# A transformer block on one core: attention's result turned by DMA in all sixteen tiles instead of six

## The chip, the core and the metric

The kernel runs on one core of a Trainium2 chip. The core has five engines that each work through their own queue in order: TensorE (PE; its weight loads are listed apart as PEld), VectorE (DVE), ScalarE (ACT), GpSimd (POOL) and SyncE (SP), which here does nothing but issue transfers. An engine whose next instruction waits does nothing else meanwhile. The metric is the time of one execution on the device in microseconds (us).

## The reference

The block has two parts, each with a residual: sliding-window attention (32 heads of 16 columns, each position looks at itself and at seven others two, four, ... fourteen positions back), then an MLP with a squared ReLU.

```python
S, D, H, Dh, W, dil, F = 2048, 512, 32, 16, 8, 2, 1792
q, k, v = heads_of(layernorm(x) @ wqkv)
logits = einsum("bhsd,bhswd->bhsw", q, k[window]) * Dh ** -0.5     # masked where pos < 0
o = einsum("bhsw,bhswd->bhsd", softmax(logits), v[window])
h = x + o.reshape(B, S, D) @ wo
r = relu(layernorm(h) @ w1 + b1)
out = h + (r * r) @ w2 + b2
```

All matrix products are made from values split into a high and a low part (a number = high + low): a product is the sum of high x high, low x high and high x low.

## The kernel before, in words

The 2048 positions are 16 tiles `t` of 128. Attention is made for pairs of tiles, `s = t // 2`. The MLP runs over groups of four tiles, `u = 0 ... 3`; `i = t % 4` is a tile's place in its group. While PE works on the QKV products of tiles 4 to 15 (`first_phase`) and then on the MLP of groups 0 to 2 (the loop over `u`), DVE and POOL make attention beside it; DVE multiplies and reduces (`dots`, `weigh`), and POOL sums the weighed values (`add_up`, L411).

Each tile goes this way: attention's result `o` (positions in partitions) is turned so that its columns lie in partitions, and split into `oh` and `ol`; the product with `wo` follows (`wo_product`, PE, into one of PSUM's banks); `h_add` (L639, DVE) adds the residual and starts the statistics of the second layernorm, either on DVE (`norm_stats`, L158 and L159) or, for the tiles in `AS`, on ACT (`act_stats`, L181 to L183); POOL finishes them with three small operations; ACT normalises (`h_norm`, L200, result `hn`); `hn` is turned and split into `hh` and `hl` for the MLP. `add_b2` (POOL) and `spill` (a DMA) put h aside until its group is finished.

There are two ways to turn a tile:

- on PE: `o_T` and `h_T` make four transposes into PSUM; ACT copies the high part from there (`hi_T`), DVE subtracts for the low part (`lo_T`, L150).
- by DMA, for the `o` of the tiles in `OV` and the `hn` of the tiles in `HV`: ACT sorts the halves of the 32-bit words into two planes (`turn_split`, L594, tile `pl`), SP issues a DMA transpose (`turn_dma`, L598), ACT puts the halves together again (`turn_join`, L603), and the split into high and low follows from there. `o_split` and `o_join` are these steps for `o`, `h_split`, `turn_join` and `h_parts` for `hn`.

The order of every engine's queue is written by a planner while the program is built. The program is a row of slots. In a slot first PE's work is written (the slot's body), then `end_slot` writes the tasks that are due in the slot (`at(delta, ...)`), then as many steps of attention as the planner thinks fit beside PE's work (`pump`), then the tasks that are to come behind them (`after(delta, ...)`):

```python
def end_slot(pe):
    now["pe"] += pe
    run(due)
    pump()
    run(late)
    now["slot"] += 1
```

`pump` goes on while DVE's planned time is less than PE's: `now["dve"] < now["pe"]`. Each step of attention is charged with its planned time times one of the factors in `SLOW` (first phase, u = 0, u = 1 and 2), the other work of DVE with `dve(...)`: 0.69 for a tile's `ol`, 0.7 for `h_add`, 0.93 for `norm_stats`, 1.0 for `HOLD`. PE is charged 0.44 for the transposes of a tile and 2.73 for a product. A weighed value's sum (`add_up`) is written only when the next step is drawn. `pump(until=s)` draws steps until attention of pair `s` is written in full.

In `first_phase` a slot is half a QKV product, and `k` counts the half-slots of its last two rounds from 0 (negative before). `OK`, `HK`, `OT`, `WO`, `HT` say at which `k` tile t's steps come. The x tiles 14 and 15 are normalised (ACT, `x_norm`) at k = 5 and 6 and transposed (PE, `x_T`) at k = 7 and 8. In this phase four PSUM banks take turns for the products.

In the loop over `u` a slot `p` holds one block `mlp1(u, f)` of the hidden layer (PE, tile `mm`, 12 matmuls), and from the fourth slot on `mlp2` (tile `acc`, 12 matmuls) of the block three slots earlier; p = 14 to 16 have `mlp2` alone. Two PSUM banks take turns for `mm`, `wo` and the transposes of this stage, so that a tile's bank is that of the one before the last. The relu that empties `mm` (`hidden`, L846, ACT) is due one slot later. `todo[p]` holds what a slot does for the next group's tiles: `OP`, `WP`, `HP` give the slots by `i`. Tiles with i = 0, 1 are split at p = 6, 7, joined two slots later, and multiplied with `wo` at p = 9, 10; tiles with i = 2, 3 are turned on PE at p = 12, 13 and multiplied at p = 13, 14 (for u = 2 one less).

Of the kernel before, what the change touches and what calls it, by code (L numbers as in the profile page):

```python
# [28 lines left out]
NEG = -4.0e9  # L29
ROWS = 15  # L30
LAG = 3
AS = (4, 5, 8, 9, 12, 13)
OV = (4, 5, 8, 9, 12, 13)
HV = (4, 5, 8, 9, 12, 13)
SLOW = 1.01, 1.10, 1.06
DELAY = 3
WJ = 2
XT = (9, 11), (7, 8)
OT = 4, 5, 10, 12
WO = 7, 9, 13, 15  # L40
HT = 20, 20, 21, 23
OK = (-6, -2, 4), (-5, -1, 5), (3, 6, 10), (4, 7, 12)
HK = (12, 15, 18), (14, 16, 19)
W2 = (18,)
LH = 3, 4, 10, 11
OP = 6, 7, 12, 13
# [12 lines left out]
def block_kernel(ctx, tc, x, wqkv, wo, w1, b1, w2, b2, out):  # L59
# [154 lines left out]
        for d, src in parts(tr, h_dst):  # L214
            hi(d, src)

    def lo_T(tr, h_dst, l_dst):
        for (d, src), h in zip(parts(tr, l_dst), h_dst):
            lo(nc.vector, d, src, h)
            dve(0.16 + 0.53 / len(h_dst))  # L220

    def mm3(ps, lh, ll, rh, rl, mid=None, at_=2 * KB, lows_last=False):

# [388 lines left out]
    def o_join(t):  # L612
        turn_join(("o", t))
        tr = planes.pop(("o", t))
        if t % R == RI:
            ohl = att.tile([P, 2, KB, P], F32R, name="ohl", tag="o", bufs=3)
            oT[t] = ohl[:, 0], ohl[:, 1]
        else:
            oT[t] = row("oh", (P, KB, P), F32R), row("ol", (P, KB, P), F32R)
        hi_T(tr, [oT[t][0]])  # L620
        after(0, lo_T, tr, [oT[t][0]], [oT[t][1]])

    def h_split(t):
        turn_split(("h", t), hn.pop(t))
# [33 lines left out]
    def wo_product(t, slots):  # L658
        ps = turn["mm"].tile("wo")
        oh, ol = oT.pop(t)  # L660
        mm3(ps, lambda k: oh[:, k, :], lambda k: ol[:, k, :],
            lambda k: wo_h[:, k, :], lambda k: wo_l[:, k, :], lows_last=t in OV)
        for n, (fn, a) in zip(slots, ((h_add, (t, ps)), (h_norm, (t,)), (add_b2, (t,)),
                                      (spill, (t,)))):
            (after if fn in (h_norm, spill) else at)(n + (fn is add_b2), fn, *a)

# [311 lines left out]
    def first_phase(t0):  # L980
        def chores(m):
            if t0 + 3 < 16:
                if m in (0, 2):
                    at(0, x_stats, t0 + 2 + m // 2)

                early = t0 == 12
                if m + early in (6, 7):
                    at(0, x_norm, t0 - 4 + m + early)
                if m in XT[early]:
                    x_T(t0 + 2 + XT[early].index(m))  # L990
            if t0 + 5 < 16 and m in (6, 9):
                at(0, load_x, t0 + 2 + m // 3)
            if jobs and m % 3 == 0:
                at(0, weight_job)
            k = t0 // 2 * 12 - 72 + m
            if k == 19:
                dve(HOLD)
            for t in range(R):
                if k == OT[t]:
                    at(0, load_h, t)  # L1000
                    if t not in OV:
                        o_T(t)
                if t in OV and k in OK[t]:
                    at(0, (o_split, lambda t: turn_dma(("o", t)), o_join)[OK[t].index(k)], t)
                if t in HV and k in HK[t]:
                    at(0, (h_split, lambda t: turn_dma(("h", t)),
                           lambda t: turn_join(("h", t)))[HK[t].index(k)], t)
                if k == WO[t]:
                    wo_product(t, (1, 3, 4, 6))
                    now["pe"] += 2.73  # L1010
                if k == HT[t]:
                    (at(0, h_parts, t) if t in HV else h_T(t))
            if k in W2:
                at(0, load_w2, W2.index(k))

        def half(m):
            end_slot(1.37)
            chores(m)

        for n in range(6):  # L1020
            chores(2 * n)
            qkv_of(t0 + n % 2, n // 2, lambda: half(2 * n + 1))
            end_slot(1.37)
# [41 lines left out]
    for u in range(R - 1):  # L1065
# [11 lines left out]
        for i in js:  # L1077
            t = R * (u + 1) + i
            if not end:
                a = i // 2 if u == 2 else 0  # L1080
                o0 = OP[i] - a
                if t in OV:
                    turned = [(o0, at, 0, o_split, t), (o0, after, 0, turn_dma, ("o", t)),
                              (o0 + 2, at, 0, o_join, t)]
# [26 lines left out]
        for p in range(FB + LAG):  # L1111
            more = 0.0
            if p == FB:
                run(due)
                dve(HOLD)
            if u < 2 and p == FB - 2:
                dve(HOLD)
            for fn, *a in sorted(todo.get(p, []), key=lambda x: x[0] is wo_product):
                fn(*a)
                more += 2.73 if fn is wo_product else 0.0  # L1120
            if p < FB:
                mlp1(u, fs[p])
                more += 2.73
                if first:
                    at(0, split_w2, p)
                    if p + 1 < FB:
                        load_w2(p + 1)
            q = p - LAG
            if q >= 0:
                f = fs[q]  # L1130
                mlp2(u, f, acc, js, q == 0, q == FB - 1,
                     (lambda: half(p)) if p in halves else None)
                more += 2.74
                if f < 12 and (need or first and p < FB - LAG):
                    free.append(place.pop(f))
                    if need:
                        at(1, fetch, need.pop(0))
            end_slot(more)
# [85 lines left out]
```

## Time and profile before

| | |
|---|---|
| median of 3 runs (lowest to highest) | 512.38 us (511.91 to 513.16) |
| profiled execution | 512.31 us, its span 510.5 us |
| PE busy | 501.9 us, 98% |
| DVE, POOL, ACT busy | 376.7, 351.2, 290.9 us |
| granted clock of PE, mean over the span | 0.999 |
| transposes of `o` on PE / by DMA | 40 in 10 tiles / 6 tiles |
| transposes of `hn` on PE / by DMA | 40 in 10 tiles / 6 tiles |

The span goes from the first to the last instruction. Busy times of different engines lie beside each other, and add up to more than the span. A row of a timeline or of the chain of waits begins with its start in us from the span's start and its length in us; a bracket at its end tells how long the engine was idle before it and whose work ended that. Rows of groups have the number of instructions, busy us and mean ns of one, and the idle time of the engine just before them.

### The profile page before, as it was taken

The page shows a single profiled execution, that of the slowest core. Times are in us where ns is not written, and L with a number is a line of the kernel's source. Part 1 is how long each engine was busy: PE and PEld are TensorE (multiplying, and loading weights), DVE is VectorE, ACT ScalarE, POOL GpSimd, SP SyncE. Part 2 cuts the span into 40 slices and gives each one's busy share as a digit, 9 for nine tenths or more (in the row PEclk, how much of TensorE's full clock was granted, in tenths as well). Part 3 has the DMA queues.
Part 4 walks back from the last instruction along what each step waited for, and adds up shares of the span by engine and source line. Part 5 has one row for each costly group of instructions (what it writes and reads, how often), then busy time and mean ns, then how long its engine had stood idle before and what let it go on. Part 6 is the DMA issues. An engine that isn't in the chain of part 4 may idle for free. (4 is left out here: it accounts for less than half of the span.)

```text
span 510.5 us, 7598 instructions
## 1 busy us (share of the span) xinstructions
PE 501.9 (98%) x2460; PEld 424.4 (83%) x2460; DVE 376.7 (74%) x512; ACT 290.9 (57%) x552; POOL 351.2 (69%) x430
## 2 busy tenths in 40 slices
PE   7999999999999999999999999999999999999997
PEld 6999788888888888888888878888888888998986
DVE  5479899988998899788879979899963046832233
ACT  4634686767434767485364557264564737666541
POOL 4714799895786798786778768776897364685610
PEclk9999999999999999999999999999999999999999
DMA  8678998989677889666587955767672172444112
GB/s 264 180 225 203 256 295 299 271 285 274 204 225 214 276 301 272 200 199 174 182 253 217 226 166 163 202 199 249 207 152 67 52 217 84 160 142 133 62 42 83
DMA packets 100912, 100.52 MB, mean 197 GB/s; under 512 B 21000, under 2 KB 69384, under 8 KB 100872
## 3 DMA queue, kind: packets, MB, share of 16 engines
q1 hardware_dynamic: 99928, 99.52, 65.4%
q10 hardware_dynamic: 944, 0.52, 0.3%
q8 instruction: 19, 0.31, 0.3%
q14 instruction: 21, 0.17, 0.1%
HBM read 72.65 MB, written 24.25 MB: 190 GB/s over the span
## 5 line engine op out<-in xcount | busy, mean ns | idle before, releaser
L411 POOL TENSOR_TENSOR pr<-pr 128x512 f32<-128x512 f32 (+1 forms) x128 | 132.5, 1035 | 45.7 <-DVE pr L354 40.3
L232 PE MATMUL mm<-big_l,w_h 128*128 128x512 f32 x336 | 88.7, 390 | 0.0
L354 DVE TENSOR_TENSOR pr<-ex,v 128x1024 f32<-128x1024 f32 x64 | 78.2, 1222 | 12.8 <-POOL o L411 6.5
L343 DVE TENSOR_TENSOR pr<-qp,k 128x1024 f32<-128x1024 f32 x64 | 76.9, 1202 | 5.6 <-ACT qp L272 5.5
L377 DVE TENSOR_REDUCE ex<-pr 128x64 f32<-128x1024 f32 x64 | 78.4, 1226 | 1.9
L232 PEld LDWEIGHTS mm<-big_l,w_h 128*128 128x128 f32 x336 | 62.8, 188 | 13.0
L150 POOL TENSOR_TENSOR rl<-r,rh 128x512 fp32r<-128x512 f32 x42 | 56.2, 1339 | 19.6 <-ACT rh L147 16.5
L232 PE MATMUL mm<-big_h,xl 128*128 128x512 f32 (+1 forms) x208 | 56.0, 379 | 0.2 <-DVE xl L150 0.2
L232 PE MATMUL mm<-big_h,xh 128*128 128x512 f32 (+1 forms) x208 | 53.5, 378 | 0.7 <-ACT xh L147 0.7
L232 PE MATMUL mm<-big_l,xh 128*128 128x512 f32 (+1 forms) x208 | 52.8, 375 | 0.0
L870 PE MATMUL acc<-big_l,rh 128*128 128x512 f32 x190 | 52.2, 390 | 0.0
L870 PE MATMUL acc<-big_h,rh 128*128 128x512 f32 x190 | 52.1, 391 | 0.0
L501 ACT COPY y<-mm 128x512 f32<-128x512 f32 (+1 forms) x52 | 28.6, 552 | 41.2 <-PE mm L232 33.0
L870 PE MATMUL acc<-big_h,rl 128*128 128x512 f32 x190 | 51.7, 389 | 0.0
L846 ACT ACTIVATE r<-mm,b_sb 128x512 f32<-128x512 f32 x42 | 28.8, 685 | 32.4 <-PE mm L232 32.3
L232 PE MATMUL mm<-big_l,w_l 128*128 128x512 f32 x168 | 45.0, 389 | 0.0
L232 PEld LDWEIGHTS mm<-big_h,xh 128*128 128x128 f32 x208 | 37.6, 188 | 7.0 <-ACT xh L147 1.5
L232 PEld LDWEIGHTS mm<-big_l,xh 128*128 128x128 f32 x208 | 38.2, 188 | 6.1 <-POOL big_l L150 0.2
L232 PEld LDWEIGHTS mm<-big_h,xl 128*128 128x128 f32 x208 | 37.2, 188 | 5.8 <-DVE xl L150 0.6
L870 PEld LDWEIGHTS acc<-big_h,rl 128*128 128x128 f32 x190 | 35.7, 188 | 7.5
L870 PEld LDWEIGHTS acc<-big_l,rh 128*128 128x128 f32 x190 | 35.5, 188 | 7.4
L870 PEld LDWEIGHTS acc<-big_h,rh 128*128 128x128 f32 x190 | 34.9, 188 | 6.7
(160 smaller groups left out, 904.1 us busy)
## 6 DMA issues: line engine op xcount, KB each, us to landing
k<-qkv_d SPq DMA_DIRECT2D x48, 288.0 KB, 2.8
v<-qkv_d SPq DMA_DIRECT2D x48, 288.0 KB, 3.2
qkv_d<-y SPq DMA_DIRECT2D x18, 512.0 KB, 4.2
big_l<-w2l_d SPq DMA_DIRECT2D x24, 256.0 KB, 3.0
xt<-in_A_x_dram SPq DMA_DIRECT2D x16, 256.0 KB, 4.6
q<-qkv_d SPq DMA_DIRECT2D x32, 128.0 KB, 4.7
h<-in_A_x_dram SPq DMA_DIRECT2D x16, 256.0 KB, 3.9
h_d<-h SPq DMA_DIRECT2D x16, 256.0 KB, 3.2
```

Of the source, the lines that this page charges most:

```text
L150: eng.tensor_tensor(out=dst, in0=src, in1=h, op=ALU.subtract)
L232: nc.tensor.matmul(ps, l(k), r(k), start=(n == 0), stop=(n == 3 * KB - 1))
L343: nc.vector.tensor_tensor(out=pr.rearrange("p i w h d -> p i w (h d)"), in0=qps["now"][:, j % 2].unsqueeze(2).to_broadcast([P, RI, W, GC]) ...
L354: nc.vector.tensor_tensor(out=p2, in1=vwin, op=ALU.mult, in0=e1[:, :, :, j * GH:(j + 1) * GH].unsqueeze(4).to_broadcast([P, RI, W, GH, DH]))
L377: nc.vector.tensor_reduce(out=lf[:, :, :, j * GH:(j + 1) * GH], in_=pr, axis=X, op=ALU.add)
L411: nc.gpsimd.tensor_tensor(out=dst, in0=p2[:, :, :w], in1=p2[:, :, w:2 * w], op=ALU.add)
L501: nc.scalar.copy(y[:, :, t % RI * GC:(t % RI + 1) * GC], ps[:, :j * GC].rearrange("p (j c) -> p j c", j=j))
L846: nc.scalar.activation(r, ps, AF.Relu, bias=b1_sb[:, f:f + 1])
L870: nc.tensor.matmul(acc[j], l[:, j * P:(j + 1) * P], w[f], start=(first and n < len(js)), stop=(last and n >= len(terms) - len(js)))
```

## The change

- `OV` holds all 16 tiles: the results of tiles 0 to 3, 6, 7, 10, 11, 14 and 15 are now turned by DMA too. `HV` has tiles 0 and 1 in addition. `AS` has tiles 0 to 3 in addition, so that their statistics are ACT's.
- `ol` of all tiles made by DMA is made by POOL (`lo_T` with `nc.gpsimd`), written behind the slot's attention steps.
- In `first_phase` the DMA follows the split in the same slot, behind the pump; `OK` and `HK` have two entries (split, join). Tiles 0 and 1 are split at k = -6, -5 and joined at 3, 4; tiles 2 and 3 are split at 3, 4 and joined at 10, 11.
- In the MLP loop tiles with i = 2, 3 are split two slots sooner than they were transposed (p = 10, 11) and joined where those transposes stood (p = 12, 13).
- The product with `wo` of these tiles comes behind `mlp1` of its slot and ahead of `mlp2`, instead of ahead of both. `h_add` of the tiles with i = 0, 1 comes behind the slot's attention steps; with i = 2, 3 it stays ahead of them. The order of a product's terms puts `ol` last for all tiles in `OV`.
- The factors in `SLOW` are 1.08 and 1.04 instead of 1.10 and 1.06 from u = 0 on.

```diff
@@ -29,18 +29,18 @@
 NEG = -4.0e9
 ROWS = 15
 LAG = 3
-AS = (4, 5, 8, 9, 12, 13)
-OV = (4, 5, 8, 9, 12, 13)
-HV = (4, 5, 8, 9, 12, 13)
-SLOW = 1.01, 1.10, 1.06
+AS = (0, 1, 2, 3, 4, 5, 8, 9, 12, 13)
+OV = tuple(range(16))
+HV = (0, 1, 4, 5, 8, 9, 12, 13)
+SLOW = 1.01, 1.08, 1.04
 DELAY = 3
 WJ = 2
 XT = (9, 11), (7, 8)
 OT = 4, 5, 10, 12
 WO = 7, 9, 13, 15
 HT = 20, 20, 21, 23
-OK = (-6, -2, 4), (-5, -1, 5), (3, 6, 10), (4, 7, 12)
-HK = (12, 15, 18), (14, 16, 19)
+OK = (-6, 3), (-5, 4), (3, 10), (4, 11)
+HK = (11, 18), (13, 19)
 W2 = (18,)
 LH = 3, 4, 10, 11
 OP = 6, 7, 12, 13
@@ -214,10 +214,11 @@
         for d, src in parts(tr, h_dst):
             hi(d, src)
 
-    def lo_T(tr, h_dst, l_dst):
+    def lo_T(tr, h_dst, l_dst, eng=nc.vector):
         for (d, src), h in zip(parts(tr, l_dst), h_dst):
-            lo(nc.vector, d, src, h)
-            dve(0.16 + 0.53 / len(h_dst))
+            lo(eng, d, src, h)
+            if eng is nc.vector:
+                dve(0.16 + 0.53 / len(h_dst))
 
     def mm3(ps, lh, ll, rh, rl, mid=None, at_=2 * KB, lows_last=False):
 
@@ -618,7 +619,7 @@
         else:
             oT[t] = row("oh", (P, KB, P), F32R), row("ol", (P, KB, P), F32R)
         hi_T(tr, [oT[t][0]])
-        after(0, lo_T, tr, [oT[t][0]], [oT[t][1]])
+        after(0, lo_T, tr, [oT[t][0]], [oT[t][1]], nc.gpsimd if t in tuple(range(16)) else nc.vector)
 
     def h_split(t):
         turn_split(("h", t), hn.pop(t))
@@ -662,7 +663,8 @@
             lambda k: wo_h[:, k, :], lambda k: wo_l[:, k, :], lows_last=t in OV)
         for n, (fn, a) in zip(slots, ((h_add, (t, ps)), (h_norm, (t,)), (add_b2, (t,)),
                                       (spill, (t,)))):
-            (after if fn in (h_norm, spill) else at)(n + (fn is add_b2), fn, *a)
+            late_ = fn in (h_norm, spill) or fn is h_add and t in OV and R <= t and t % R < RI
+            (after if late_ else at)(n + (fn is add_b2), fn, *a)
 
 
 
@@ -1001,10 +1003,17 @@
                     if t not in OV:
                         o_T(t)
                 if t in OV and k in OK[t]:
-                    at(0, (o_split, lambda t: turn_dma(("o", t)), o_join)[OK[t].index(k)], t)
+                    if k == OK[t][0]:
+                        at(0, o_split, t)
+                        after(0, turn_dma, ("o", t))
+                    else:
+                        at(0, o_join, t)
                 if t in HV and k in HK[t]:
-                    at(0, (h_split, lambda t: turn_dma(("h", t)),
-                           lambda t: turn_join(("h", t)))[HK[t].index(k)], t)
+                    if k == HK[t][0]:
+                        at(0, h_split, t)
+                        after(0, turn_dma, ("h", t))
+                    else:
+                        at(0, turn_join, ("h", t))
                 if k == WO[t]:
                     wo_product(t, (1, 3, 4, 6))
                     now["pe"] += 2.73
@@ -1078,7 +1087,7 @@
             t = R * (u + 1) + i
             if not end:
                 a = i // 2 if u == 2 else 0
-                o0 = OP[i] - a
+                o0 = OP[i] - a - (2 if i >= RI and t in OV else 0)
                 if t in OV:
                     turned = [(o0, at, 0, o_split, t), (o0, after, 0, turn_dma, ("o", t)),
                               (o0 + 2, at, 0, o_join, t)]
@@ -1115,7 +1124,11 @@
                 dve(HOLD)
             if u < 2 and p == FB - 2:
                 dve(HOLD)
-            for fn, *a in sorted(todo.get(p, []), key=lambda x: x[0] is wo_product):
+            body = todo.get(p, [])
+            behind = [x for x in body if x[0] is wo_product and x[1] in OV]
+            for fn, *a in sorted(body, key=lambda x: x[0] is wo_product):
+                if [fn, *a] in behind:
+                    continue
                 fn(*a)
                 more += 2.73 if fn is wo_product else 0.0
             if p < FB:
@@ -1125,6 +1138,9 @@
                     at(0, split_w2, p)
                     if p + 1 < FB:
                         load_w2(p + 1)
+            for fn, *a in behind:
+                fn(*a)
+                more += 2.73
             q = p - LAG
             if q >= 0:
                 f = fs[q]
```

## The prediction

> **What bounds the kernel now.** I read the page's first part, then TensorE's waits, then the chain. In the page a share of 98% stands for PE. In the waits (engine, waiting line <- releaser: us in total, times, longest) there is hardly one.
>
> ```profile
> span 510.5 us, 7598 instructions
> PE 501.9 (98%) x2460; PEld 424.4 (83%) x2460; DVE 376.7 (74%) x512; ACT 290.9 (57%) x552; POOL 351.2 (69%) x430
> PE wo L232 <- DVE ol L150: 1.2, 2, 0.6
> PE tr L205 <- ACT xt L200: 0.4, 1, 0.4
> ```
>
> So PE sets the time, and only two things move the end: less work on PE, or a new wait of PE. The chain of waits in order of time (start, us, what) shows PE's pace: 2.72 us for a group of 12 matmuls (a hidden block "mm", its second product "acc", or an output product "wo"), 0.44 for the four transposes of a tile.
>
> ```profile
> 322.92 0.44 PE tr L205 x4
> 323.36 2.77 PE wo L232 x12
> 326.13 2.72 PE mm L232 x12
> 328.85 2.72 PE acc L870 x12
> ```
>
> The profiled execution took 512.31 us, 0.07 below the median of the three runs; the sum is made against it.
>
> **What leaves PE.** Ten tiles of the result and residual tiles 0 and 1 lose their transposes: 12 x 0.44 = 5.3 us, all on the bound. The two stalls of wo on `ol` (1.2 us, row above) should go as well, since ol leaves DVE and the products of the later tiles come one group later. Gain 6.5 us.
>
> [...]
>
> **What comes instead.** Columns: line, engine, operation, out<-in, count | busy us, mean ns | idle before; the fifth row ends in us to landing.
>
> ```profile
> L603 ACT COPY pl<-o 128x1024 uint16<-128x1024 uint16 x6 | 7.0, 1168 | 1.3 <-DMA o<-pl 1.3
> L594 ACT COPY pl<-o 128x1024 uint16<-128x1024 uint16 x6 | 6.2, 1040 | 0.0
> L150 POOL TENSOR_TENSOR rl<-r,rh 128x512 fp32r<-128x512 f32 x42 | 56.2, 1339 | 19.6 <-ACT rh L147 16.5
> L639 DVE TENSOR_TENSOR h<-wo,h 128x512 f32<-128x512 f32 x16 | 11.0, 686 | 26.3 <-PE wo L232 26.3
> o<-pl SPq DMA_TRANSPOSE x6, 4.3
> ```
>
> ACT gets 12 splits and 12 joins (12 x 2.21 = 26.5 us) and four tiles' statistics. POOL gets 16 `ol` at about 1.34 (21 us). DVE loses them. SP issues 12 transposes more, with a landing of 4.3 us; split and join of a moved tile lie at least two MLP slots (2 x 5.44 us) or six half-slots apart, so I cost DMA at nothing, covered by that distance. If SP were late by more than it, the join would hold ACT; the row's 1.3 us in two of six joins says how little this did so far. By totals all fits, so what counts is order in the queues, place by place.
>
> **A. ACT at k = 3 and 4.** Into ACT's queue ahead of the normalisation of x tile 14 come join 0, split 2 (k = 3), join 1 with its `oh`, split 3 (k = 4). ACT, then PE, in the timeline (start, us, engine, line):
>
> ```profile
> 120.15 0.36 ACT L272 COPY qp<-q 128x256 f32<-128x256 f32 x1
> 120.67 0.59 ACT L501 COPY y<-mm 128x512 f32<-128x512 f32 x1 [0.16 <-PE mm L232]
> ...
> 122.40 0.82 ACT L200 ACTIVATE xt<-xt,rs 128x512 f32<-128x512 f32 x1
> 123.12 0.57 ACT L147 CAST oh<-tr 128x512 fp32r<-128x512 f32 x1
> 125.50 0.60 PE L205 MATMUL tr<-ident,xt 128*128 128x128 f32 x4
> ```
>
> ACT has no gap here but 0.16. Added: 2 x 1.17 + 2 x 1.04 + 0.57 = 5.0, less some 0.08 per instruction that neighbours overlap (0.36 after 120.15 would reach 120.51, and similar), and the gap: 4.4. The normalisation then ends at 122.40 + 0.82 + 4.4 = 127.6. PE, two transposes earlier, wants the tile at 125.50 - 0.88 = 124.6. Stall 3.0 us; bounds 0 (ACT had run ahead) and 4.
>
> **B. Statistics of tiles 0 to 3** move from DVE to ACT, which then waits for the addition of h. Four PSUM banks turn in this stage, so I take 0, bound 2.
>
> **C. The products of tiles 6, 7 and 10, 11.** Here the change adds a circle. Call E the end of wo(6). `h_add(6)` stays ahead of the attention steps of its slot (p = 13), and the product now comes one group later, so DVE stands at E and all attention of that slot behind it. POOL's `ol(7)` is put behind the sums of that slot's steps, and the sums wait for DVE. wo(7), one slot on, needs `ol(7)`. Rows of DVE for the statistics and for one such run of steps, and of POOL for one sum:
>
> ```profile
> 235.20 0.69 DVE L639 TENSOR_TENSOR h<-wo,h 128x512 f32<-128x512 f32 x1 [1.41 <-PE wo L232]
> 235.92 0.69 DVE L158 BATCH_NORM_STATS2 st<-h 128x6 f32<-128x512 f32 x1
> 236.65 0.18 DVE L159 BATCH_NORM_AGGREGATE mv<-st 128x2 f32<-128x6 f32 x1
> ...
> 287.87 0.41 DVE L366 TENSOR_REDUCE sm<-ex 128x32 f32<-128x256 f32 x1
> 288.32 1.23 DVE L377 TENSOR_REDUCE ex<-pr 128x64 f32<-128x1024 f32 x1
> 289.45 0.34 DVE L383 RECIPROCAL sm<-sm 128x32 f32<-128x32 f32 x1
> 289.71 1.16 DVE L343 TENSOR_TENSOR pr<-qp,k 128x1024 f32<-128x1024 f32 x1
> 290.79 0.42 DVE L371 TENSOR_TENSOR ex<-ex,sm 128x256 f32<-128x256 f32 x1
> 291.30 1.22 DVE L354 TENSOR_TENSOR pr<-ex,v 128x1024 f32<-128x1024 f32 x1
> ...
> 287.44 2.12 POOL L411 TENSOR_TENSOR pr<-pr 128x512 f32<-128x512 f32 x2
> 289.64 0.46 POOL L411 TENSOR_TENSOR o<-pr 128x128 f32<-128x128 f32 x1
> ```
>
> Which steps fall there follows from the planner's charges. Up to that slot DVE loses 4 x 0.69 + 4 x 0.93 (tiles 0 to 3) + 4 x 0.69 (tiles 4 to 7) = 9.2, PE 8 x 0.44 = 3.5, and the factor 1.08 for 1.10 yields 0.9 over some 47 us: attention stands 6.6 us, about six steps, further on. The slot p = 13 of u = 0 then draws: sum, reduce, reciprocal, k product, weighing, reduce. One sum goes out with the last step, by a margin of 0.36 in the planner's account; in u = 1 (reduce, k product, weighing, reduce, k product) with room.
>
> u = 0: statistics to E + 1.6; the steps from 287.87 to 291.30 + 1.22 take 4.65, so E + 6.25; the sum (287.44 to 290.10) 2.7: E + 9.0; `ol(7)` 1.34: E + 10.3. wo(7) starts at E + 2.72 and wants `ol` for its last third, at E + 4.5. Stall 5.8. u = 1: steps of 1.23 + 1.16 + 1.22 give E + 5.2, `ol(11)` at E + 9.2: 4.7. In u = 2 attention is over by then, none. C = 10.5; bounds 0 and, with two sums ahead of each `ol`, 16.
>
> **D. Tiles 4, 5, 8, 9, 12, 13.** These take statistics on ACT. The product now follows mm(p), and the next mm needs the PSUM bank that mm(p)'s relu frees; that relu stands behind the statistics in ACT's queue, and they wait for the product. ACT's rows:
>
> ```profile
> 297.87 0.63 ACT L181 ACTIVATE scrap<-h 128x512 f32<-128x512 f32 x1 [1.17 <-DVE h L639]
> ...
> 299.49 0.18 ACT L183 ACTIVATION_READ_ACCUMULATOR scrap<-h,nm 128x1 f32 x1
> 299.89 0.69 ACT L846 ACTIVATE r<-mm,b_sb 128x512 f32<-128x512 f32 x1 [0.21 <-PE mm L232]
> ```
>
> h_add 0.69, statistics 1.8 (297.87 to 299.67), relu 0.69, hand-overs 0.15: 3.3 after the product's end; one acc of 2.72 covers it. 0.6 x 6 = 3.6 us. `h_add` is also put behind its slot's attention; DVE comes in time if it is a microsecond ahead, else up to 2 us a tile more: bounds 0 and 12.
>
> **Moved at no cost:** late splits two slots sooner (the heads are summed by then by the account above, cover about four steps); turn_dma right behind the split; the factors themselves (they only place steps).
>
> Sum: 512.3 - 6.5 + 3.0 + 0 + 10.5 + 3.6 = 522.9.
>
> **The rivals.**
> - *No sum stands ahead of `ol`* (C is 0): 512.3 - 6.5 + 3.0 + 3.6 = 512.4, not slower. Place: POOL at p = 13. It decides if `ol(7)` is there by E + 4.5, thus if the slot draws a step less. For: the margin of 0.36 in u = 0. Against: u = 1 has room.
> - *ACT and POOL hide everything*: 505.8. For: 43% and 31% idle; TensorE waited 1.2 us for this work so far. Against: so far 10 tiles had no copies in ACT's queue, and C and D are circles, which idle time does not shorten.
> - *The clock falls in the new stalls.* PE's last matmul ends by 507.1; the windows of the end (us, busy of PE, PEld, DVE, ACT, POOL, clock, DMA share, GB/s):
>
> ```profile
> 508.00:509.00 1.00, 0.00 (x0) 0.00 (x0) 0.00 (x0) 0.00 (x0) 0.00 (x0) 1.00 0.77 270
> 509.00:510.50 1.50, 0.00 (x0) 0.00 (x0) 0.00 (x0) 0.00 (x0) 0.00 (x0) 0.60 0.00 0
> ```
>
>  Between 2 and 3.4 us of idleness the clock falls. No gap before was so long; those of C would be. If the next group then runs at half speed, 2.72 us each: 522.9 + 5.4 = 528.3. [...]
>
> **The numbers.** Forecast 0.60 (516 to 526 alone: half of D and C's shorter run, or DVE late), clock 0.13, no sum ahead 0.12, all hidden 0.15. Slower takes the first two, 0.73. Faster: all hidden and 0.05 of the no-sum case (A or D at their lower ends), 0.20; same 0.07. A measurement here tells 0.3%, 1.5 us, from no change. Time 523. The range of 8 in 10 goes from 508, halfway into the hidden case, to 529.
>
> **What would show it.** Right: PE busy near 496, and waits of PE on `POOL ol` (two, about 5 us each), on `ACT xt` about 3, on `ACT r` about 0.6 six times. Wrong: PE's waits still near 5 us in sum; then the hidden rival holds. If wo never waits for POOL, C failed; if DVE's wait in h_add (26.3) does not grow, its first link failed.

## The result, and the profile after

The changed kernel takes 554.19 us (median; 552.31 to 555.68), the kernel before 512.58 beside it: a ratio of 1.081 [1.077, 1.085]. Forecast were 523.0 with a range of 508 to 529. The direction held and the size did not: 41.6 us were lost, not 10.6.

The page of the changed kernel begins with the span and with each engine's busy time:

```profile
span 551.5 us, 7571 instructions
PE 509.8 (92%) x2412; PEld 426.6 (77%) x2412; DVE 367.6 (67%) x488; ACT 321.5 (58%) x596; POOL 367.4 (67%) x446
```

Two numbers carry the result (PE's idle time is the span less its busy time). PE's idle time rose from 510.5 - 501.9 = 8.6 to 551.5 - 509.8 = 41.7 us, by 33.1. Its busy time rose too, from 501.9 to 509.8, though 48 transposes (5.3 us) are gone: matmuls became slower by some 13.2 in sum. 33.1 + 13.2 - 5.3 = 41.0, the difference of the spans. PE's waits of the changed kernel (engine, waiting line <- releaser: us in total, times, longest):

```profile
PE mm L233 <- ACT r L848: 10.9, 6, 3.7
PE wo L233 <- POOL ol L150: 10.1, 2, 5.6
PE tr L205 <- ACT xt L200: 7.6, 2, 7.2
PE mm L233 <- ACT y L502: 3.2, 2, 2.6
```

The three rows forecast are there (D, C, A in this order). The second has the size forecast; the first and third are two to three times theirs. The fourth, 3.2 us for the evacuation of `y`, falls into B, which the sum had at 0. Lines of the changed kernel stand one or two further down than before (L233 was L232, L848 was L846).

**C came as worked out.** The timeline of the changed kernel (start, us, engine, line), PE, then DVE, then POOL:

```profile
252.50 1.07 PE L233 MATMUL wo<-wo_h,ohl 128*128 128x512 f32 x4
266.80 2.07 PE L233 MATMUL wo<-wo_h,ol 128*128 128x512 f32 x4 [5.64 <-POOL ol L150]
...
256.67 0.69 DVE L640 TENSOR_TENSOR h<-wo,h 128x512 f32<-128x512 f32 x1 [6.29 <-PE wo L233]
261.63 1.23 DVE L355 TENSOR_TENSOR pr<-ex,v 128x1024 f32<-128x1024 f32 x1
...
262.93 2.06 POOL L412 TENSOR_TENSOR pr<-pr 128x512 f32<-128x512 f32 x2 [5.06 <-DVE pr L355]
265.48 1.26 POOL L150 TENSOR_TENSOR ol<-pl,oh 128x512 fp32r<-128x512 f32 x1
```

(`ohl` is one tile for both parts, high and low, where i = 2.) h_add(6) waits for wo(6), the attention steps for h_add(6), one sum on POOL for the steps, `ol(7)` for the sum, and wo(7) for `ol(7)`: the stall is 5.64, forecast 5.8; that of wo(11) is 4.46, forecast 4.7.

**A has a second cause.** In the timeline ACT, ahead of the copies that were counted, stands idle for a load, and SP's rows show why that load is late:

```profile
121.35 0.57 ACT L147 CAST w_h<-raw 128x448 fp32r<-128x448 f32 x1 [4.04 <-DMA raw<-in_B_w_dram]
130.86 0.81 ACT L200 ACTIVATE xt<-xt,rs 128x512 f32<-128x512 f32 x1
...
110.01 1.37 SPq L599 DMA_TRANSPOSE o<-pl  x1
112.10 1.25 SPq L599 DMA_TRANSPOSE o<-pl  x1
114.78 0.88 SPq L441 DMA_DIRECT2D xt<-in_A_x_dram  x1
115.71 0.47 SPq L552 DMA_DIRECT2D raw<-in_B_w_dram  x1
```

The same two loads in the kernel before, without transposes ahead of them:

```profile
110.67 0.62 SPq L440 DMA_DIRECT2D xt<-in_A_x_dram  x1
111.34 0.46 SPq L551 DMA_DIRECT2D raw<-in_B_w_dram  x1
```

They go out 4.1 and 4.4 us later.

**D is the ACT order plus a late DVE.** The timeline of the changed kernel after wo(4), which ended at 223.23:

```profile
225.90 0.63 DVE L640 TENSOR_TENSOR h<-wo,h 128x512 f32<-128x512 f32 x1
226.62 0.63 ACT L181 ACTIVATE scrap<-h 128x512 f32<-128x512 f32 x1 [3.40 <-DVE h L640]
228.33 0.67 ACT L848 ACTIVATE r<-mm,b_sb 128x512 f32<-128x512 f32 x1
229.05 1.20 PE L233 MATMUL mm<-big_l,w_h 128*128 128x512 f32 x4 [3.10 <-ACT r L848]
```

The row of h_add names no wait: DVE was busy and came 2.67 us late. In u = 2, where attention is over and DVE idle, the same stall is 0.54 and 0.48, as forecast (0.6). Two rows of DVE's own waits grew, in the changed kernel:

```profile
DVE h L640 <- PE wo L233: 65.8, 8, 14.9
DVE pr L344 <- ACT qp L273: 26.5, 9, 5.4
```

and before:

```profile
DVE h L639 <- PE wo L232: 26.3, 12, 6.5
DVE pr L343 <- ACT qp L272: 5.5, 4, 3.5
```

The first is the sign that was named for C's first link, and it came. The second is attention's own copy of q into PSUM, which goes through ACT, behind splits, joins and the statistics of tiles 0 to 3. Neither row explains the late h_add. Between 167.34 and h_add(4) at 225.90 DVE has no wait over 1.3 us, and between 268.91 and h_add(8) at 329.03, which came 3.31 us late, none over 1.0; the longest wait of this stage for the copy of q (4.98, until 334.69) comes after h_add(8). DVE was busy for 51.8 of the 56 us up to h_add(4); which part of the change put it behind is not shown.

### The profile page after: what moved, and what is told of

Read it like the earlier page. It is cut to its first block, busy times and chain, and to the rows that moved or that the text cites. A ratio compares the mean times of both kernels' runs of the same rounds, so it can differ in the third digit from the quotient of the medians.

```text
span 551.5 us, 7571 instructions
## 1 busy us (share of the span) xinstructions
PE 509.8 (92%) x2412; PEld 426.6 (77%) x2412; DVE 367.6 (67%) x488; ACT 321.5 (58%) x596; POOL 367.4 (67%) x446
## 5 line engine op out<-in xcount | busy, mean ns | idle before, releaser
L233 PE MATMUL mm<-big_l,w_h 128*128 128x512 f32 x336 | 90.1, 395 | 11.6 <-ACT r L848 10.9
L344 DVE TENSOR_TENSOR pr<-qp,k 128x1024 f32<-128x1024 f32 x64 | 76.9, 1202 | 27.8 <-ACT qp L273 26.5
L233 PEld LDWEIGHTS mm<-big_l,w_h 128*128 128x128 f32 x336 | 63.0, 189 | 27.6 <-ACT r L848 13.6
L150 POOL TENSOR_TENSOR rl<-r,rh 128x512 fp32r<-128x512 f32 x42 | 54.6, 1303 | 22.9 <-ACT rh L147 18.1
L233 PE MATMUL mm<-big_h,xh 128*128 128x512 f32 (+1 forms) x208 | 53.7, 380 | 3.4 <-ACT y L502 2.6
L233 PE MATMUL mm<-big_h,xl 128*128 128x512 f32 (+1 forms) x208 | 56.5, 383 | 0.2 <-DVE xl L150 0.2
L640 DVE TENSOR_TENSOR h<-wo,h 128x512 f32<-128x512 f32 x16 | 10.9, 682 | 65.8 <-PE wo L233 65.8
L872 PE MATMUL acc<-big_h,rh 128*128 128x512 f32 x190 | 53.8, 401 | 0.0
L872 PE MATMUL acc<-big_l,rh 128*128 128x512 f32 x190 | 53.5, 398 | 0.0
L233 PE MATMUL mm<-big_l,xh 128*128 128x512 f32 (+1 forms) x208 | 53.0, 376 | 0.0
L848 ACT ACTIVATE r<-mm,b_sb 128x512 f32<-128x512 f32 x42 | 28.7, 683 | 32.4 <-PE mm L233 26.3
L233 PEld LDWEIGHTS mm<-big_h,xh 128*128 128x128 f32 x208 | 38.0, 189 | 10.5 <-ACT y L502 3.0
L233 PE MATMUL mm<-big_l,w_l 128*128 128x512 f32 x168 | 45.6, 394 | 0.0
L233 PEld LDWEIGHTS mm<-big_l,xh 128*128 128x128 f32 x208 | 38.6, 190 | 6.1
L233 PEld LDWEIGHTS mm<-big_h,xl 128*128 128x128 f32 x208 | 37.9, 191 | 6.0 <-DVE xl L150 0.6
L872 PEld LDWEIGHTS acc<-big_h,rh 128*128 128x128 f32 x190 | 36.1, 194 | 7.2
```

Source lines behind the costliest of these rows:

```text
L150: eng.tensor_tensor(out=dst, in0=src, in1=h, op=ALU.subtract)
L233: nc.tensor.matmul(ps, l(k), r(k), start=(n == 0), stop=(n == 3 * KB - 1))
L344: nc.vector.tensor_tensor(out=pr.rearrange("p i w h d -> p i w (h d)"), in0=qps["now"][:, j % 2].unsqueeze(2).to_broadcast([P, RI, W, GC]) ...
L640: nc.vector.tensor_tensor(out=h, in0=ps, in1=h, op=ALU.add)
L848: nc.scalar.activation(r, ps, AF.Relu, bias=b1_sb[:, f:f + 1])
L872: nc.tensor.matmul(acc[j], l[:, j * P:(j + 1) * P], w[f], start=(first and n < len(js)), stop=(last and n >= len(terms) - len(js)))
```

## Experiments: parts of the change undone

Ratios are to the kernel before, which ran beside each version (511.7 to 512.6 us), with their 95% intervals; the changed kernel has 1.081.

**`ol` on POOL ahead of the slot's attention.**

```
-        after(0, lo_T, tr, [oT[t][0]], [oT[t][1]], nc.gpsimd if ... )
+        at(0, lo_T, tr, [oT[t][0]], [oT[t][1]], nc.gpsimd if ... )
```

> The changed kernel with one edit: POOL's `ol` of every tile is issued ahead of the slot's attention steps, not behind them. Circle theory (C): the sums stood ahead of `ol(7)` and `ol(11)`, so the two stalls of wo (5.64 at 261.16, 4.46 at 365.26) go. Circle and clock: with them go the two stretches of 6.83 at half speed (265.1, 367.5), 3.4 us each: 554.2 - 10.1 - 6.8 = 537.3. Waits alone, with the halves caused by something else: 544. If `ol` was late for another reason (the join, ACT's cast): about 554.

Measured 548.48, 1.070 [1.066, 1.074]. No row of PE waiting for POOL's `ol` is left, so the sums ahead of it were the cause of C. But only 5.7 of the 16.9 us hoped for came back. The waits of this run show where they went:

```profile
PE mm L233 <- ACT y L502: 5.8, 2, 5.2
PE tr L205 <- ACT hn L200: 4.1, 3, 2.7
```

The wait for `y` grew by 2.6, one for `hn` of 4.1 is new: all on ACT. Half speed (a granted clock of 0.50) moved as well: it lasts 23.9 us in this run, 27.3 in the changed kernel.

**Tiles 0 to 3 as before.**

```
-AS = (0, 1, 2, 3, 4, 5, 8, 9, 12, 13)
-OV = tuple(range(16))
-HV = (0, 1, 4, 5, 8, 9, 12, 13)
+AS = (4, 5, 8, 9, 12, 13)
+OV = tuple(range(4, 16))
+HV = (4, 5, 8, 9, 12, 13)
```

> The changed kernel with tiles 0 to 3 as before (transposes of PE, statistics on DVE; AS, OV, HV without 0 to 3). Theory: the stalls of A and B (7.22 at 124.50, 1.64 at 148.22, 2.56 at 159.68, 0.68 at 175.98 = 12.1) go, and with them the half-speed stretches of 6.83 at 128.6 and 3.41 at 162.7 (5.1 us lost); six groups of transposes come back (6 x 0.44 = 2.6): 554.2 - 12.1 - 5.1 + 2.6 = 539.6. Rival: these stalls come from the order of the later work that is still there (splits and joins of other tiles, SP's queue), and only part goes: above 547.

Measured 539.16, 1.052 [1.050, 1.055]: 15.0 us back, 14.6 expected. A and B hang on these four tiles; no stall over 0.6 us is left between 10 and 210 us. That the sum fits so well is in part luck, since later waits changed too: those of wo for POOL's `ol` fell from 10.1 to 2.5, and those for ACT's relu grew from 10.9 to 17.5 (5.6 of them now ahead of wo). DVE's wait for the copy of q fell from 26.5 to 16.8 here, and the relu waits of D did not fall with it.

**The product ahead of mlp1 again.**

```
-            behind = [x for x in body if x[0] is wo_product and x[1] in OV]
+            behind = []
```

> The changed kernel with the output product ahead of its slot's mlp1 again (the list `behind` is empty). Theory (D and C as forecast): the six waits of mm on ACT's relu (10.9 in all, one of which led to 3.41 at half speed, 1.7 lost) go; wo(7) and wo(11) then have one group of 2.72 more between them and wo(6), wo(10), so the C stalls shrink to 2.9 and 1.7, and are too short to halve the clock (6.8 back): 554.2 - 10.9 - 1.7 - 5.4 - 6.8 = 529.4. Rival, D alone: 541.6. Rival, the waits come from h_add put behind the attention (DVE late), whatever the place of the product: above 550.

Measured 542.87, 1.060 [1.058, 1.062]: 11.3 us back. PE's waits for ACT's relu are gone, and the C stalls are 2.91 and 1.84, as expected (2.9, 1.7). That they would be too short to halve the clock was my assumption, and the run does not show it: the run's mean clock of 0.984 over 541.4 us makes some 17 us at half speed, 27.3 in the changed kernel, where the theory left 10.2. In place of the waits for relu stand a wait of 3.15 for h_add at 335.5 and waits for POOL's `ohl`:

```profile
PE wo L233 <- POOL ol L150: 6.5, 4, 2.9
PE wo L233 <- POOL ohl L150: 3.8, 2, 3.3
```

So the waits of D hang on the product's place; about half of what it frees is taken by the next queue.

**PE kept busy in three stalls.** Matmuls with a matrix of zeros, and transposes of the identity, fill the wait; nothing comes sooner.

```
+FILL = {7: 22, 11: 17}
+FILL_X = {14: 60}
+            for n in range(FILL[t]):
+                nc.tensor.matmul(ps, nil, wo_h[:, n % KB, :], start=False, stop=False)
+        for n in range(fill):
+            nc.tensor.transpose(tr[:, n % KB, :], ident, ident)
```

> The changed kernel, in which PE is kept busy in three of its stalls: 60 transposes of the identity ahead of those of x's tile 14 (6.6 us of the 7.22), and 22 and 17 matmuls with a matrix of zeros (5.0 of 5.64 and 3.9 of 4.46) in wo(7) and wo(11) ahead of the terms of `ol`. What is computed stays the same, and nothing that PE waits for comes sooner. Clock theory: idleness of PE halves the clock, so the stretches of 6.83 at half speed at 128.6, 265.1 and 367.5 go, 3.4 us each: 554.2 - 10.2 = 544. Rival: the half speed is due to something other than PE's idleness (the time goes with load or the place): 554.

Measured 551.75, 1.077 [1.075, 1.080]. Windows of the changed kernel around the stall of wo(7) (us, then busy of PE, PEld, DVE, ACT, POOL, then the granted clock, DMA share and GB/s):

```profile
261.70:265.10 3.40, 0.00 (x0) 0.00 (x0) 2.38 (x2) 0.63 (x2) 2.01 (x3) 1.00 0.64 153
265.10:268.50 3.40, 1.70 (x4) 1.42 (x5) 0.00 (x0) 0.00 (x0) 3.23 (x5) 0.50 0.46 135
268.50:271.90 3.40, 3.40 (x9) 2.62 (x9) 2.92 (x5) 1.32 (x3) 3.00 (x6) 0.50 0.45 119
```

and of this run:

```profile
263.50:266.90 3.40, 3.40 (x16) 2.60 (x14) 1.47 (x2) 0.00 (x0) 2.93 (x4) 1.00 0.76 234
266.90:270.30 3.40, 2.69 (x12) 2.11 (x12) 1.28 (x2) 0.00 (x0) 3.13 (x6) 1.00 0.36 89
```

The clock stays at 1.00 in all three filled places, which in the changed kernel had 20.5 us at 0.50, so there PE's idleness halved it. But the time fell by 2.4, not by 10.2. Part of the sum was wrong: within the three stretches PE was idle for 3.15, 1.69 and 2.21 us, so half speed cost at most (20.5 - 7.1) / 2 = 6.7. Of the rest, what is gained after x's tile 14 is lost at once, since wo(2) still waits for `ohl` until 149.2 (149.9 in the changed kernel). New in this run are a wait of 1.26 at 184.2 and a stretch of 3.41 at half speed at 229.3, behind 3.41 us of which PE was idle for 2.6. So the run shows what halved the clock in these three places; what half speed costs by itself it does not isolate.

**The weight block split a slot later.**

```
-        at(5, split)
+        at(6, split)
```

> The changed kernel with each weight block split six slots after its load, not five. It tests why the stall at 124.50 was 7.22 and not 3.0. SP theory: the two transposes of tiles 0 and 1 (issued at 110.01 and 112.10, 1.37 and 1.25 of SP) hold the loads behind them, the weight block's load goes out at 115.71 instead of 111.34, and ACT's 4.04 of waiting for it stands ahead of the copies that x's tile 14 waits behind. Then ACT's wait for the load goes, the stall is some 3.2 and the time 4 less: 550. Rival: ACT has that much work in any order, or what follows (POOL's `ohl(2)` at 149.88) takes it up: the stall or the ones behind it grow, 553 to 555.

Measured 554.01, 1.081 [1.080, 1.083]: no gain, the rival. ACT no longer waits for the weight load, but 1.76 for the load of x's tile 15 right ahead of it in SP's queue; the stall is 5.98.

**h_add ahead of attention for all tiles.**

```
-            late_ = fn in (h_norm, spill) or fn is h_add and t in OV and R <= t and t % R < RI
+            late_ = fn in (h_norm, spill)
```

> The changed kernel with h_add ahead of its slot's attention steps for all tiles (the clause for late h_add taken out). Theory for D: of the 10.9 us that mm waits for ACT's relu in six places, 3.6 are the order of ACT (0.6 each, as in u = 2) and 7.3 come from DVE, which reached h_add(4) 2.67 and h_add(8) 3.3 us after the end of the product; then the waits shrink to 3.6 and the time to 547, or 545 with the half speed at 333.4. Rival: attention behind a waiting h_add is late instead, its sums hold `ol(5)` and `ol(9)` as they hold `ol(7)`, and wo waits for POOL: 554 or more.

Measured 556.81, 1.086 [1.082, 1.089]: the rival's time, 2.6 above the changed kernel, with intervals that overlap. The waits of mm for relu fell only to 8.1 (2.4 more stand ahead of wo), and `ohl(6)` is waited for 4.1. Late h_add is not what costs here, whether it gains is not clear of noise, and DVE's lateness isn't cured by this order.

**The old factors.**

```
-SLOW = 1.01, 1.08, 1.04
+SLOW = 1.01, 1.10, 1.06
```

> The changed kernel with the old pacing factors (1.01, 1.10, 1.06). Forecast of the prediction: factors only place steps, nothing is gained or lost: 552.7 to 555.7. Rival: with 2% less charged to each step DVE is given more than it has time for; over the some 260 us of attention in slots charged at 1.08 that is about 5 us of DVE, the lateness of h_add(4) and h_add(8) goes, and the time falls by some 5: 549.

Measured 544.79, 1.062 [1.060, 1.064]: 9.4 us back for 0.02, the dearest line of the change for its size. In POOL's timeline of this run two sums stand ahead of `ohl(6)` (the second is shown), and none between the slot's other work and `ol(7)`:

```profile
255.20 2.08 POOL L412 TENSOR_TENSOR pr<-pr 128x512 f32<-128x512 f32 x2
257.37 0.45 POOL L412 TENSOR_TENSOR o<-pr 128x128 f32<-128x128 f32 x1
257.78 1.26 POOL L150 TENSOR_TENSOR ohl<-pl,ohl 128x512 fp32r<-128x512 f32 x1
...
260.22 1.28 POOL L150 TENSOR_TENSOR rl<-r,rh 128x512 fp32r<-128x512 f32 x1
261.46 1.29 POOL L150 TENSOR_TENSOR ol<-pl,oh 128x512 fp32r<-128x512 f32 x1
```

`ol(7)` is ready at 262.75, not 266.74, and wo(7) does not wait. For tile 7 that is the rival "no sum stands ahead of `ol`": one step less in the slot decides, and the factor decides that. It does not hold elsewhere: wo(6) now waits 3.00 for `ohl(6)`, and wo(11) still waits 2.44 for `ol(11)`, behind one sum. The waits for relu fell to 8.2, with 1.2 ahead of wo.

**Only six late blocks.** Tiles 0 to 3, the product's place, h_add and the factors all as before; left are tiles 6, 7, 10, 11, 14, 15 by DMA, their early splits, and `ol` on POOL (of the edits above, those to tiles 0 to 3, to the product's place, to h_add and to the factors together).

> Of the change only the six late blocks are left (attention's result of tiles 6, 7, 10, 11, 14, 15 by DMA, their splits two slots sooner, `ol` of every DMA tile on POOL behind the slot's attention): tiles 0 to 3 as before, product ahead of mlp1, h_add ahead of attention, old factors. Theory, the priced terms: 512.4 - 6 x 0.44 transposes - 1.2 of waits + 4.7 of C (2.9 and 1.8 as in the run with the product first): 513. Additive from the parts undone (15.0 for tiles 0 to 3, 11.3 for the product's place): 528 or less. Rival: POOL and ACT with the copies of six more blocks are late by themselves: 520 or more, with waits of PE on POOL `ol` and ACT `oh`.

Measured 527.56, 1.029 [1.026, 1.032]. Both the additive sum and the rival fit; 513 is out. PE's waits:

```profile
PE wo L233 <- POOL ol L150: 5.9, 4, 3.4
PE wo L233 <- POOL ohl L150: 4.2, 1, 4.2
PE wo L233 <- ACT ohl L147: 2.8, 1, 2.8
```

## Experiments: parts of the change alone

**Six late blocks, `ol` on POOL ahead of attention** (the run above with the first edit).

> The run with six late blocks only (527.6), with POOL's `ol` ahead of its slot's attention steps. There PE waited 12.9 us for POOL's `ol`, with 13.7 us of half speed behind three of the waits. Theory: the place behind the sums makes `ol` late, so these waits go: 527.6 - 12.9 = 514.7, 512 with a part of the half speed. Rival: POOL then stands at `ol` until ACT has cast `oh`, the sums behind it come late and with them the next split, as in the run with `ol` ahead, which gained 5.7 where 10.1 of waits went: 522.

Measured 518.81, 1.014 [1.012, 1.016], between the two. The waits for POOL's `ol` and `ohl` fell from 10.1 to 0.6, those for ACT's `ohl` rose from 2.8 to 6.1. (The 12.9 us that the expectation gives to POOL hold these 2.8 of ACT.)

**Six late blocks, `ol` on DVE** (`nc.gpsimd if ...` left out).

> The run with six late blocks only (527.6), with `ol` of all DMA tiles on DVE and charged in the planner, as before. What is left of the change is then six blocks by DMA instead of PE, split two slots sooner. Theory: POOL's `ol` carries the whole rest (15.2 over before), and the six blocks bring their transposes: 512.4 - 6 x 0.44 - 1.2 = 508.6, up to 512 if ACT's copies cost something. Rival: ACT's split and join of six more blocks, or the earlier split that waits for the heads, cost as well: 518 or more, with waits of PE on ACT `oh` or DVE `ol`.

Measured 518.98, 1.014 [1.011, 1.016]: the rival. POOL's `ol` carried 8.6 of 15.2; the blocks cost the rest, with `ol` now late on DVE:

```profile
PE wo L233 <- DVE ol L150: 4.2, 2, 2.7
PE wo L233 <- DVE ohl L150: 1.6, 1, 1.6
```

**Only `ol` on POOL, in the kernel before.**

```
-        after(0, lo_T, tr, [oT[t][0]], [oT[t][1]])
+        after(0, lo_T, tr, [oT[t][0]], [oT[t][1]], nc.gpsimd)
```

> The kernel before with one edit: `ol` of its six DMA tiles (4, 5, 8, 9, 12, 13) on POOL behind the slot's attention, uncharged, instead of on DVE. Theory: the move to POOL is dear by itself; in the run with six late blocks these tiles' products waited 1.21, 3.43 and 0.56 for it, and DVE's freed 0.69 each is filled with attention: 516 to 520. Rival: POOL is late only where tiles 6, 7, 10, 11 by DMA add their `ol` to the same slots: 511 to 514.

Measured 523.08, 1.022 [1.020, 1.023]: above even the theory. POOL's timeline ahead of wo(9)'s last third shows two sums in front of `ol(9)`:

```profile
301.15 2.11 POOL L412 TENSOR_TENSOR pr<-pr 128x512 f32<-128x512 f32 x2 [1.37 <-DVE pr L355]
303.34 0.46 POOL L412 TENSOR_TENSOR o<-pr 128x128 f32<-128x128 f32 x1
303.76 2.07 POOL L412 TENSOR_TENSOR pr<-pr 128x512 f32<-128x512 f32 x2
305.91 0.45 POOL L412 TENSOR_TENSOR o<-pr 128x128 f32<-128x128 f32 x1
306.32 1.26 POOL L150 TENSOR_TENSOR ol<-pl,oh 128x512 fp32r<-128x512 f32 x1
```

PE waits 3.43 there, 1.20 and 3.33 in two other places. The 10.8 of span divide into 5.5 of idle time (8.6 to 14.1) and 5.3 of slower matmuls; the two stretches at half speed, 6.83 and 3.41 with 1.05 us of idleness in them, account for 4.6 of that. No run fills these waits, so what the time would be without half speed is not shown.

**Only the factors, in the kernel before.** First lower, as in the change:

> The kernel before with one edit: the pacing factors 1.01, 1.08, 1.04. The old factors in the changed kernel gained 9.4. Theory: a factor lower by 0.02 hands DVE more steps than it has time for, in any kernel of this build: 516 to 521. Rival: it costs only where DVE stands behind late products and POOL's `ol` behind the sums; the kernel before has room: 511 to 514.

Measured 514.89, 1.006 [1.005, 1.008]: 3.2 us, between the two; waits for DVE's `ol` rise from 1.2 to 3.2. Then higher (1.01, 1.12, 1.08), as the control for a run below:

> The kernel before with factors 1.01, 1.12, 1.08: the control for the run above. Theory: its two waits for DVE's `ol` (0.61 and 0.56) go and nothing else: 511.2 to 512. Rival: attention is behind where the transposes of its result want it, and PE waits for the heads: 514 or more.

Measured 518.08, 1.011 [1.007, 1.014]: the rival's time, by another wait. PE does not wait for the heads but 4.5 us for DVE's `ol`; ahead of the longest of these (3.14) DVE had stood 2.03 and 1.50 for loads of v. Either way is dearer; in the kernel before the factor stands at a place where 0.02 up costs 5.6 and 0.02 down 3.2.

## Experiments: the size of A, and what holds the six blocks

**The transposes of tiles 0 and 1 issued three half slots later.**

```
-                        after(0, turn_dma, ("o", t))
+                        after(3 if t < 2 else 0, turn_dma, ("o", t))
```

> The changed kernel, the DMA transposes of attention's result of tiles 0 and 1 issued three half slots later. SP theory: at 110.01 and 112.10 they held the loads of x's tile 15 and of a weight block by some 4.1 us; ACT then waited 4.04 for the one, and with that wait covered 1.76 for the other. With the transposes behind these loads ACT has no such wait, the stall at 124.50 falls from 7.22 to 3 to 4 (the copies alone, as forecast), and the time to 551, or less than that if POOL's `ohl(2)` at 149.88 doesn't take it up. Rival: the stall is ACT's own work (waiting 1.74 for POOL's sum at split 0, then copies): it stays over 5.5, and the time at 554.

Measured 551.28, 1.076 [1.073, 1.079], between the two. The stall falls from 7.22 to 4.85, so SP's queue is worth 2.4 of it. ACT still waits 1.68 for the weight load:

```profile
119.57 0.57 ACT L147 CAST w_h<-raw 128x448 fp32r<-128x448 f32 x1 [1.68 <-DMA raw<-in_B_w_dram]
```

With that taken off, some 3.2 would be left, near the 3.0 forecast for the copies; no run took it off. In the changed kernel ACT stands 1.74 at split 0 for POOL's sum, with the evacuations behind it; that this wait is what delays SP's stores and with them the load is my reading and was not tried by itself.

**A join one slot sooner, its transpose ahead of the slot's loads** (six blocks, `ol` on DVE).

```
-(o0, after, 0, turn_dma, ("o", t)), (o0 + 2, at, 0, o_join, t)
+(o0, at if i >= RI else after, 0, turn_dma, ("o", t)), (o0 + (1 if i >= RI else 2), at, 0, o_join, t)
```

> The run with six late blocks and `ol` on DVE (519.0), in which the late blocks' transposes are issued ahead of the slot's loads of k and v and joined one slot sooner. Theory: the join of tiles 6 and 10 stood behind two splits of h in ACT's queue (227.87 and 230.92 in the run with `ol` ahead), so wo waited 1.22 and 1.65 for `ohl`; these go: 516. Rival: loads of k and v behind a transpose that waits for the split come late, DVE with them: 519 or more.

Measured 520.23, 1.014 [1.010, 1.018]. The waits for `ohl` are gone; 3.62 for ACT's `hn` are new, and h_add(6) comes 5.0 us after its product. No gain: the rival's time. Whether its late loads are the reason is not shown.

**Factors 1.12 and 1.08** (six blocks, `ol` on DVE).

> The run with six late blocks and `ol` on DVE (519.0), with factors 1.01, 1.12, 1.08. Theory: what is left is DVE's pace; the planner gives DVE more than it can do by the time `ol` is wanted (waits of PE on DVE's `ol` and `ohl`: 2.66, 1.65, 1.57, and 3.41 at half speed). With 2% more charged these go: 519.0 - 5.9 - 1.7 = 511.4. Rival: attention that is further behind makes the splits late (they wait for the heads) or runs past the last group: 517 or more.

Measured 526.01, 1.025 [1.020, 1.030]: the rival's time, as in the control. PE's waits for the parts `oh`, `ol` and `ohl` grew from 7.0 to 12.6 us where they were to go.

**The late join ahead of the splits of h** (six blocks, `ol` ahead on POOL).

```
-            for fn, *a in sorted(body, key=lambda x: x[0] is wo_product):
+            for fn, *a in sorted(body, key=lambda x: (x[0] is wo_product, h_split in x)):
```

> The run with six late blocks and POOL's `ol` ahead (518.8), with the join of a late tile ahead of the splits of h in the same slot. Theory: wo(6) and wo(10) waited 2.85 and 3.29 for ACT's `ohl`, whose join stood behind two splits of 1.04 and a wait of 2.00; ahead of them it waits only for its DMA (landed at 229.46, wanted at 230.88 less 1.8 of copies): the waits fall to some 0.5 each, and the 3.41 at half speed goes: 518.8 - 5.1 - 1.7 = 512. Rival: ACT waits for the DMA with the splits of h and relu behind it, and wait moves there, as it moved when the join was a slot sooner: 517 or more.

Measured 519.83, 1.016 [1.013, 1.018]: the rival. The wait for ACT's `ohl` falls from 6.1 to 3.1, that for `hn` rises from 1.7 to 2.6 and that for POOL's `ol` and `ohl` from 0.6 to 3.2.

**Two blocks more, where attention is over.** The kernel before with tiles 14 and 15 by DMA (split two slots sooner).

```
-OV = (4, 5, 8, 9, 12, 13)
+OV = (4, 5, 8, 9, 12, 13, 14, 15)
```

> The kernel before with attention's result of tiles 14 and 15 by DMA too (split two slots sooner, `ol` on DVE, old factors): the part of the change that falls where attention is over. Theory: nothing contends there, so two groups of transposes go and nothing comes: 512.0 - 0.9 = 511.1. Rival: the joins and splits in ACT's queue cost as they do for tiles 6, 7, 10, 11: 513 to 515.

Measured 511.06 against 511.78, 0.9983 [0.9968, 0.9997], 511.1 expected. It is the only version that is not slower than the kernel before: 0.7 us, with the end of the interval close to 1, less than the 0.3% that I had called telling.

## Why the prediction was right and wrong, step by step

The sum failed in what it put at nothing and in two sizes. At nothing stood the factors (9.4 us when undone), the DMA behind SP's queue (2.4), B (4.9) and slower matmuls (13.2); A and D were sized by ACT's copies alone (7.22 for 3.0, 10.9 for 3.6). Of the stalls only C was right in mechanism and size.

- *What leaves PE.* 48 matmul records fewer, as worked out. But in tiles 4 to 13 the wait for `ol` did not simply go: on POOL alone it costs 11.4 (1.022). The prediction priced `ol` on POOL only for tiles 7 and 11. The worth of the transposes shows in the run with two blocks more: eight fewer brought 0.7 us, 0.9 by the row of 0.44 for four.
- *DMA at nothing.* Wrong. It was weighed by landing against joining, which held but for 3.9 us of ACT's time ahead of two of 16 joins, and not by what stands behind a transpose in SP's queue: two of them held a load of x and one of weights by over 4 us (2.4 of PE's stall).
- *A, 3.0, bounds 0 to 4.* Measured 7.22. SP's queue is 2.4 of it, ACT's wait for a load that was left without it 1.7; the other 3.2 are near the 3.0 for the copies. Why the load is still late is not shown.
- *B, 0, bound 2.* Wrong: 1.64 + 2.56 + 0.68 = 4.9 in this stage. Statistics wait for h_add in ACT's queue, and what PE needs stands behind them: the join of tile 2 (ACT stood 3.67 for h_add(1), until 145.81) and the evacuation of `y` (1.92 for h_add(2), until 159.91). Four banks did not cover it, since h_add(2) began 6.3 us after its product (152.88, 159.14), before it 2.1 (143.93, 146.03): DVE had stood 3.76 and 1.86 us for ACT's copies for attention. So ACT delays DVE, and DVE ACT.
- *C, 10.5.* Measured 10.10, right in both places (5.64 and 4.46 for 5.8 and 4.7); the run with `ol` ahead shows the cause. Taking it away brings only 5.7, since waits on ACT grow.
- *D, 3.6, bounds 0 to 12.* Measured 10.9 within the bounds. The 0.6 for ACT's order shows alone in u = 2; the remainder is DVE late, by 2.67 and 3.31 us at tiles 4 and 8. That had been named, with up to 2 us a tile, and not taken.
- *The factors at no cost: the dearest of the terms put at nothing.* 9.4 us in the changed kernel, 3.2 in the kernel before. The prediction had used the factor to count steps in C and still called it free. For tile 7 a step more in the slot is a sum more ahead of `ol`.
- *The clock.* The rival's mechanism came, in five stretches (27.3 us at a granted clock of 0.50) instead of two. Its price of 5.4 for two was an upper one: filling three brought 2.4, with a new stretch elsewhere. PE busy, to be near 496, is 509.8, by my estimate below 10.1 of it for this reason.
- *Rivals.* "All hidden" fell. "No sum ahead" was false for the change; with the old factors it holds for tile 7 and not for tiles 6 and 11.

Where the 31 us beyond the forecast are: 4.2 in A, 4.9 in B, 7.3 in D, less 0.4 in C, 1.2 of other idle time, together 17.2 (41.7 against 8.6 - 1.2 + 17.1 = 24.5), and 13.2 of slower matmuls. The five stretches at half speed, less 7.1 us of idleness in them, give 10.1 of the 13.2; for the remaining 3 I have no row.

The parts don't add: tiles 0 to 3, the product's place and the factors taken back one at a time give 15.0 + 11.3 + 9.4 = 35.7, and together with h_add, which gave -2.6 alone, 26.6. What one queue gives back, the next takes.

It stays open which resource holds six late blocks at 519. Moving the join a slot or ahead of the splits of h, `ol` to another engine or ahead of the sums, and the pace each moved the wait elsewhere, at 519 to 526. Two blocks in the stage without attention seem to pay (0.7 us); in the stages with attention blocks did not in any form tried. It also stays open what makes DVE late in D.

## What to carry to other kernels

When work leaves the bounding engine for three others that pass work to each other in fixed orders, total idle time of these is no cover: list what stands behind each moved instruction on ACT, POOL, DVE and SP, the copies of other streams included (here attention's copy of q on ACT). A pacing factor is a cost term like any other: price it by the instructions that it pulls ahead of a waited-for one. And move first the blocks whose stage has no other traffic; here two of them brought 0.7 us, hardly clear of noise, and the whole change lost 41.6.

## What the runs showed of the hardware

The granted clock of the changed kernel is 1.00 or 0.50. Its stretches at 0.50 begin at 128.58, 162.71, 265.11, 333.37 and 367.51 and last 6.83, 3.41, 6.83, 3.41 and 6.83 us; their starts lie 34.13, 102.40, 68.27 and 34.13 apart, 10, 30, 20 and 10 times 3.413. Cut into steps of that length from the first start, the trace has PE idle for 3.41, 2.56, 3.41, 2.21 and 2.25 us in the step ahead of each stretch, and for 1.61 at most in the others at full clock up to PE's last matmul. Within the stretches the steps with 3.15, 1.69 and 2.21 us idle were followed by another at 0.50, the five without idleness by 1.00. Two stalls stand in its windows like this, the first of 2.56 us within one step, the second of 3.10 split over two:

```profile
159.30:162.70 3.40, 0.83 (x4) 0.42 (x3) 3.31 (x5) 2.21 (x6) 3.15 (x6) 1.00 1.01 179
162.70:166.10 3.40, 3.40 (x10) 2.61 (x9) 1.92 (x3) 1.28 (x4) 3.16 (x5) 0.50 0.79 232
...
224.10:227.60 3.50, 1.85 (x9) 1.19 (x7) 3.47 (x7) 0.93 (x3) 3.27 (x5) 1.00 0.82 228
227.60:231.00 3.40, 1.95 (x9) 1.61 (x10) 3.27 (x4) 3.33 (x6) 3.08 (x6) 1.00 0.83 252
231.00:234.40 3.40, 3.40 (x17) 2.82 (x16) 2.96 (x3) 1.81 (x4) 3.15 (x4) 1.00 0.43 144
```

Here the longer stall (3.10) kept the clock at 1.00 and the shorter one (2.56) was followed by 0.50; that this is due to where they fall is my reading, and no run moved a stall without changing it. In the kernel before the clock went to 0.50 at 509.31, 2.2 us after the end of PE's last matmul (507.13).
